# The first chunk of the projections taken in two halves of its tokens, with four weight blocks begun before the rounds

## The chip, the cores and the metric

The kernel runs on one core of a Trainium2 chip. The metric is the device time of one execution in microseconds (us), the median of several runs. Engines are named as the profile names them: PE multiplies matrices (PEld is its weight load), ACT applies functions and copies, DVE and POOL work element by element, SP only issues transfers. Each engine, and each queue of transfers, takes its instructions in the order in which they were written, and waits on semaphores for the others.

## The reference

One transformer block in float32, with S = 2048 tokens of D = 640, 32 heads of 20 and a gated layer of F = 1728:

```python
def _A_ref(x, wqkv, wo):
    qkv = (x @ wqkv).reshape(B, S, 3, H, Dh).transpose(2, 0, 3, 1, 4)
    q, k, v = qkv[0], qkv[1], qkv[2]
    p = softmax(einsum("bhqd,bhkd->bhqk", q, k) * Dh ** -0.5)
    return einsum("bhqk,bhkd->bhqd", p, v).transpose(0, 2, 1, 3).reshape(B, S, D) @ wo
def _B_ref(x, w_gate, w_up, w_down):
    return (silu(x @ w_gate) * (x @ w_up)) @ w_down
h  = x + _A_ref(layernorm(x), wqkv, wo)
h2 = h + _B_ref(layernorm(h), w_gate, w_up, w_down)
```

The layer norm has no weights: `(x - mean) / sqrt(var + 1e-5)`.

## The kernel before, in words

**Stages.** The projections (q, k, v) take the first 320 us, attention follows until about 1430 us, and the gated layer fills the rest. All engines' instructions are laid down in program order (`manual_schedule`); nothing is reordered later.

**Precision.** A float32 operand is held as two fast-format parts, `hi` (a copy by ACT) and `lo` (the difference, by DVE or POOL); `split` makes them. A product is the sum of three: `z_hi·w_hi`, `z_lo·w_hi`, `z_hi·w_lo`, so a weight block of 128 columns needs 15 steps (three parts by `ND` = 5 slices of D).

**Projections.** Tokens go in four chunks of 512 (`CH`), each of four tiles of 128 (`TPC`). A chunk has 18 work items: ten blocks `("block", m)` of 128 columns (even m are keys, odd m queries) and eight value parts. `slot` counts work items, 18 per chunk, 72 in all. In `rounds`, a block's matmuls are cut into a half over rows 0 to 63 and a half over rows 64 to 127; the second halves follow 20 steps behind (`LAG`), so that in the steady state two halves run side by side. `keep` takes a finished block out of PSUM: ACT copies, DVE or POOL takes the difference, the result `e` is stored to DRAM (`q_d`, `k_d`) through POOL's queue (`store`); for the last block of the last chunk through SP's queue.

**Row maxima in between.** Softmax needs each row's maximum. Part of them is computed during the projections (`early`, from `items` that are loaded back from DRAM with `load_items`, by SP's queue): `max_four` multiplies, ACT takes a relu, PE adds, DVE reduces. `visit`, called after each step of `rounds`, decides from modelled engine clocks (`clock`, `takes`, `held`, `given`) whether one of these goes in. `stored_at` says from which slot on a group's keys and queries count as stored.

**The hand-over to attention.** Unit 0 is the first of 32 (head group, query chunk) units. When the last of its maxima is reduced, `max_all(0)` puts `neg` in place. Two work items later, or behind the last one when the items run out, `max_finish(0)` transposes `neg` on PE, splits it (ACT, then DVE: tile `m`) and lets SP write it into rows of `q_stk` by four transfers (L352). The first score of attention (L1297) reads those rows.

**The first chunk.** `load_x(0)` loads the four token tiles, then `load_w` the weights, 256 columns (two blocks) each, into a ring of four `raw` tiles. `norm(0)` computes mean and variance of all four tiles (DVE, L137, L138), the reciprocal root by a bit trick and three Newton steps (`rstd_steps`, L111), and normalises each tile (L574). Meanwhile PE multiplies a tile by the identity three times (`warm`, L820). `flip_tokens` transposes a tile on PE (L628) and splits it into `z_hi`, `z_lo`. `first_blocks` then computes blocks 0 and 1 with full-height matmuls over 256 tokens (L720), and `rounds` begins with block 2 (L667).

## Time and profile before

| | |
|---|---|
| median of 3 runs | 2004.37 us (2004.31 to 2004.98) |
| the profiled execution: its time | 2004.65 us |
| its span, first to last instruction | 2002.9 us, so 1.75 us lie around it |
| PE busy | 1981.1 us, 99% |
| DVE, ACT, POOL busy | 1604.4, 1430.4, 786.2 us |
| granted clock of TensorE | 0.999 |

A line of a timeline reads: start in us from the span's start, duration in us, engine, source line, operation, output<-inputs, shape, number of merged instructions; in brackets the idle time of the engine just before and what ended it. A line without brackets followed its predecessor at once. Lines of SPq are the issues of transfers by SP's queue. For merged rows the duration runs from the start of the first to the end of the last. Line numbers are those of the kernel before; in the changed kernel the same line stands a few to some sixty lines further on.

### The profile page before, as it was taken

The page shows a single profiled execution, that of the slowest core. Times are in us where ns is not written, and L with a number is a line of the kernel's source. Part 1 is how long each engine was busy: PE and PEld are TensorE (multiplying, and loading weights), DVE is VectorE, ACT ScalarE, POOL GpSimd, SP SyncE. Part 2 cuts the span into 40 slices and gives each one's busy share as a digit, 9 for nine tenths or more (in the row PEclk, how much of TensorE's full clock was granted, in tenths as well). Part 3 has the DMA queues.
Part 4 walks back from the last instruction along what each step waited for, and adds up shares of the span by engine and source line. Part 5 has one row for each costly group of instructions (what it writes and reads, how often), then busy time and mean ns, then how long its engine had stood idle before and what let it go on. Part 6 is the DMA issues. An engine that isn't in the chain of part 4 may idle for free.

```text
span 2002.9 us, 41974 instructions
## 1 busy us (share of the span) xinstructions
PE 1981.1 (99%) x14792; PEld 1260.4 (63%) x14792; DVE 1604.4 (80%) x2873; ACT 1430.4 (71%) x2828; POOL 786.2 (39%) x1152
## 2 busy tenths in 40 slices
PE   8999999999999999999999999999999999999998
PEld 6999996444444444444444444455688888888887
DVE  5687778999999999999999999975478666677667
ACT  4677778999999999999999999977633221212221
POOL 6564423243252343334342111011255544844465
PEclk9999999999999999999999999999999999999999
DMA  7787563442533544435345222221268645974542
GB/s 239 258 258 258 176 208 90 129 121 97 161 104 114 150 135 130 130 111 157 120 134 161 79 73 60 77 67 59 65 207 291 235 159 180 358 243 166 199 147 93
DMA packets 197066, 310.50 MB, mean 155 GB/s; under 512 B 51368, under 2 KB 85480, under 8 KB 195832
## 3 DMA queue, kind: packets, MB, share of 16 engines
q1 hardware_dynamic: 190264, 284.21, 43.9%
q0 software_dynamic: 6496, 23.60, 3.9%
q8 instruction: 118, 1.93, 0.4%
q14 instruction: 92, 0.75, 0.1%
q10 hardware_dynamic: 96, 0.00, 0.0%
HBM read 208.11 MB, written 99.19 MB: 153 GB/s over the span
## 4 chain that ended last, share of the span: by engine, by line
PE 90%; DVE 1%; POOL 1%; ACT 1%; DMA 1%; issue 0%; SPq 0%; DVEq 0%; POOLq 0%; ACTq 0%
PE acc L1307 25%; PE ps_a L1494 15%; PE ps_one L1297 12%; PE ps_max L289 9%; PE ps_b L1588 8%; PE ps_max L261 7%; PE ps_one L667 7%; PE ps_max L228 3%; PE ps_max L1028 2%; PE ps_b L1028 1%; DMA t_d<-kept 0%; POOL h L1626 0%; DVE tmp L1709 0%; PE ps_max L1063 0%; POOL yp L102 0%
## 5 line engine op out<-in xcount | busy, mean ns | idle before, releaser
L1303 ACT ACTIVATE probs<-ps_one 128x512 f32<-128x512 f32 x2048 | 1049.2, 615 | 43.0 <-PE ps_one L1297 33.9
L267 DVE TENSOR_REDUCE found<-ps_max 128x1 f32<-128x512 f32 x980 | 630.4, 685 | 81.1 <-PE ps_max L261 63.7
L1297 PE MATMUL ps_one<-q_stk,k_stk 62*128 62x512 f32 x2048 | 571.9, 427 | 0.2 <-ACT probs L1303 0.2
L1307 PE MATMUL acc<-probs,v_stk 128*32 128x512 f32 x4096 | 546.6, 605 | 0.0
L289 PEld LDWEIGHTS ps_max<-k_stk,q_stk 60*128 60x128 f32 x984 | 181.8, 185 | 407.1 <-DVE found L267 402.7
L261 PE MATMUL ps_max<-k_stk,q_stk 60*128 60x512 f32 x980 | 392.9, 422 | 0.0
L298 DVE TENSOR_REDUCE found<-ps_max 128x2 f32<-128x512 f32 x492 | 335.1, 681 | 0.0
L289 PE MATMUL ps_max<-k_stk,q_stk 60*128 60x256 f32 x984 | 324.1, 329 | 0.0
L1297 PEld LDWEIGHTS ps_one<-q_stk,k_stk 62*128 62x128 f32 x2048 | 301.7, 184 | 20.0 <-ACT probs L1303 16.2
L1709 DVE TENSOR_TENSOR tmp<-ps_a,tmp 128x512 f32<-128x512 f32 x208 | 141.1, 689 | 119.7 <-PE ps_a L1494 94.0
L250 DVE TENSOR_REDUCE mx<-ps_max 128x2 f32<-128x512 f32 x288 | 180.7, 685 | 69.1 <-PE ps_max L228 61.8
L261 PEld LDWEIGHTS ps_max<-k_stk,q_stk 60*128 60x128 f32 x980 | 181.0, 185 | 52.1 <-DVE found L298 21.6
L1588 PE MATMUL ps_b<-halves,yp 128*128 128x320 f32 x1032 | 179.3, 308 | 2.0 <-POOL yp L102 1.2
L240 ACT ACTIVATE ps_max<-ps_max 128x512 f32<-128x512 f32 x288 | 151.4, 584 | 40.9 <-PE ps_max L228 38.9
L1588 PEld LDWEIGHTS ps_b<-halves,yp 128*128 128x128 f32 x1032 | 165.1, 188 | 18.7 <-POOL yp L102 1.5
L1494 PE MATMUL ps_a<-t,units 128*128 128x512 f32 x624 | 162.6, 396 | 0.0
L1307 PEld LDWEIGHTS acc<-probs,v_stk 128*32 128x32 f32 x4096 | 81.0, 108 | 128.5 <-issue 118.3
L102 POOL TENSOR_TENSOR yp<-y,yp 128x256 fp32r<-128x256 f32 x96 | 60.2, 627 | 188.2 <-ACT yp L101 188.2
L1494 PE MATMUL ps_a<-z,units 128*128 128x512 f32 x516 | 133.9, 394 | 0.0
L1494 PEld LDWEIGHTS ps_a<-t,units 128*128 128x128 f32 x624 | 112.5, 188 | 18.6
L1342 POOL TENSOR_TENSOR o<-o,rb 128x512 f32<-128x512 f32 x31 | 39.8, 1285 | 212.1 <-DMA q_stk<-q_d 80.0
L319 POOL CAST both<-neg 128x16 fp32r<-128x16 f32 x22 | 4.3, 197 | 299.0 <-DVE neg L309 243.5
(220 smaller groups left out, 3077.3 us busy)
## 6 DMA issues: line engine op xcount, KB each, us to landing
units<-w_d SPq DMA_DIRECT2D x186, 256.0 KB
w_d<-stage SPq DMA_DIRECT2D x106, 256.0 KB
halves<-j_d SPq DMA_DIRECT2D x70, 320.0 KB
j_d<-stage SPq DMA_DIRECT2D x42, 320.0 KB
k_stk<-k_d SPq DMA_DIRECT2D x64, 160.0 KB
q_stk<-q_d SPq DMA_DIRECT2D x64, 160.0 KB
raw<-k_d SPq DMA_DIRECT2D x62, 160.0 KB
raw<-q_d SPq DMA_DIRECT2D x54, 160.0 KB
```

The lines of the kernel that those rows point to most:

```text
L240: nc.scalar.activation(ps, ps, AF.Relu)
L250: nc.vector.tensor_reduce(mx[:, b, :, t, kc], ps.rearrange("p (j n) -> p j n", j=2), axis=AX.X, op=ALU.max,)
L261: nc.tensor.matmul(ps, queries[u][rows, pair, t * P : (t + 1) * P], keys[u // NC][rows, pair, kc * CH : (kc + 1) * CH], start=True, stop=True,
L267: nc.vector.tensor_reduce(found_of(u)[:, b, pair, t, kc : kc + 1], ps, axis=AX.X, op=ALU.max)
L289: nc.tensor.matmul(ps[:, b * CH // 2 : (b + 1) * CH // 2], queries[u][rows, pair, t * P : (t + 1) * P], keys[u // NC][rows, pair, first : ...
L298: nc.vector.tensor_reduce(found_of(u)[:, :, pair, t, column], ps.rearrange("p (b n) -> p b n", b=2), axis=AX.X, op=ALU.max,)
L1297: nc.tensor.matmul(ps, keys[u // NC][rows, p, kt * P : (kt + 1) * P], queries[u][rows, p, :], start=True, stop=True,)
L1303: nc.scalar.activation(probs[p][:, b, :], ps, AF.Exp, scale=scale)
L1307: nc.tensor.matmul(acc[32 * j : 32 * j + 32, :], values[u // NC][:, kt, j * VW : j * VW + 32], probs[j // 2][:, j % 2, :], start=(kt == 0) ...
L1494: nc.tensor.matmul(ps.rearrange("p (t n) -> p t n", t=TPC), w[k][:, i], z[k][:, :, j], start=(first and m == 0), stop=(last and m == len(n ...
L1588: nc.tensor.matmul(ps, a, b, start=(n == 0), stop=(n == len(pairs) - 1))
L1709: add = lambda out, ps, x: nc.vector.tensor_tensor(out=out, in0=ps, in1=x, op=ALU.add)
```

## The change: what it does

It rewrites the first chunk's beginning and what depends on it:

- SP loads token tiles 0 and 1, then the first weights, then tiles 2 and 3, then the other weights. The matmuls by the identity are two instead of three and read tile 1.
- Statistics, reciprocal root and normalisation go by pairs of tiles (`first_tokens`), with `scalar_tensor_tensor` on two tensors (a constant tile `magic`, `r` broadcast along the row) where `norm` has `tensor_scalar`. For the other chunks `norm` stays as it is.
- Blocks 0 to 3 (not 0 and 1) are computed by `first_blocks`, with 256 tokens per matmul: for tokens 0 to 255 as soon as tiles 0 and 1 are flipped, for tokens 256 to 511 in work item 0. Blocks 2 and 3 have two PSUM banks of their own, a pool on the other side (`psum_pair`); `psum_wide` shrinks from three buffers to two. `rounds` begins with block 4.
- The `lo` parts of weight blocks 0 to 3 are made by POOL (before: DVE), and POOL's fill of `k_stk` with ones (L153) comes behind them, no longer first.
- The planner: `stored_at` is `2 * block + 5` for chunk 0, `given` starts with one entry, work items 2 and 3 of chunk 0 are empty, and each pair of first blocks advances PE's modelled clock by 3510 ns.

```diff
-        for c, name, n in ((ps_ctx, "psum_o", 2), (flip_ctx, "psum_w", 3))
+            (ps_ctx, "psum_o", 2, "left"), (flip_ctx, "psum_w", 2, "left"),
+            (pair_ctx, "psum_p", 1, "right"),
...
-                return 2 * block + 4 + (block > 0)
+                return 2 * block + 5
...
-        given = [0, 0, 0]
+        given = [0]
...
+        def first_tokens(ts, mv):
+            n = len(ts)
+            v, r, t = (pa.tile([P, n], F32, name=f"{x}_first", bufs=2) for x in "vrt")
+            var = mv[:, ts[0] : ts[-1] + 1, 1]
+            stt = nc.vector.scalar_tensor_tensor
+            stt(v, var, EPS, var, op0=ALU.add, op1=ALU.max)
+            stt(r.bitcast(I32), v.bitcast(I32), -0.5, magic[:, :n], op0=ALU.mult, op1=ALU.add)
+            for _ in range(3):
+                nc.vector.tensor_tensor(out=t, in0=r, in1=r, op=ALU.mult)
+                stt(t, t, -0.5, v, op0=ALU.mult, op1=ALU.mult)
+                stt(r, t, 1.5, r, op0=ALU.add, op1=ALU.mult)
+            for i, k in enumerate(ts):
+                stt(
+                    xs[k], xs[k], mv[:, k, 0:1], r[:, i : i + 1].to_broadcast([P, D]),
+                    op0=ALU.subtract, op1=ALU.mult,
+                )
...
-        load_x(0)
-        fill_ones(k_stk[0])
-        for i in range(4):
+        load_x(0, 0, 2)
+        load_w(0)
+        load_x(0, 2, TPC)
+        for i in range(1, 4):
             load_w(i)
         warm = ps_one()
-        for _ in range(3):
-            nc.tensor.matmul(warm, ident, xs[TPC - 1][:, :CH], start=True, stop=True)
-        for _, _, f in norm(0):
-            f()
+        for _ in range(2):
+            nc.tensor.matmul(warm, ident, xs[1][:, :CH], start=True, stop=True)
...
+        def first_low(*ms):
+            for m in ms:
+                cs = slice(m * P, (m + 1) * P)
+                nc.gpsimd.tensor_tensor(
+                    out=w_lo[:, :, cs], in0=first_raw[m], in1=w_hi[:, :, cs].bitcast(F32),
+                    op=ALU.subtract,
+                )
...
+        first_high(0, 1)
+        first_low(0, 1)
+        first_stats(0)
+        first_stats(1)
+        first_tokens((0, 1), moments)
+        first_stats(2)
+        flip_tokens(0)
+        flip_tokens(1)
...
+        first_high(2, 3)
+        first_low(2, 3)
+        fill_ones(k_stk[0])
+        first_blocks((0, 1), (0, 0), (0, 1), (0, 2))
+        first_stats(3)
+        first_tokens((2, 3), moments)
+        first_blocks((2, 3), (0, 0))
+        flip_tokens(2)
+        first_blocks((2,), (0, 1))
+        flip_tokens(3)
+        first_blocks((3,), (0, 1))
+        first_blocks((2, 3), (0, 2))
...
-        first = [("block", 0), ("none",)] + [("block", m) for m in range(2, 2 * ND)]
+        first = [("block", 0), ("none",), (), ()] + [("block", m) for m in range(4, 2 * ND)]
...
-                        first_blocks((0, 1), (1, 0), (1, 1), (0, 2), (1, 2))
-                        for m, ps in enumerate(firsts):
-                            keep(0, m, ps)
+                        for ms in ((0, 1), (2, 3)):
+                            first_blocks(ms, (1, 0), (1, 1), (1, 2))
+                            takes("PE", 3510)
+                            for m in ms:
+                                keep(0, m, firsts[m])
```

**Where instructions move: PE, start of the program.** `L628` and `L631` are the transposes of token tiles, `L720` and `L721` are `first_blocks`, `L667` and `L670` are `rounds`. Before:

```order
L820 MATMUL ps_two<-xt,ident 128x512 x3
L628 MATMUL ps_wide<-ident,xt 128x128 x15
L720 MATMUL ps_two<-z_hi,w_hi 128x256 x10
L628 MATMUL ps_wide<-ident,xt 128x128 x5
L720 MATMUL ps_two<-z_lo,w_hi 128x256 x10
L720 MATMUL ps_two<-z_hi,w_hi 128x256 x10
L720 MATMUL ps_two<-z_lo,w_hi 128x256 x10
L720 MATMUL ps_two<-z_hi,w_lo 128x256 x20
```

Now, to the end of the first half of blocks 2 and 3:

```order
L840 MATMUL ps_two<-xt,ident 128x512 x2
L631 MATMUL ps_wide<-ident,xt 128x128 x10
L721 MATMUL ps_two<-z_hi,w_hi 128x256 x10
L721 MATMUL ps_two<-z_lo,w_hi 128x256 x10
L721 MATMUL ps_two<-z_hi,w_lo 128x256 x10
L721 MATMUL ps_pair<-z_hi,w_hi 128x256 x10
L631 MATMUL ps_wide<-ident,xt 128x128 x5
L721 MATMUL ps_pair<-z_lo,w_hi 128x256 x5
L631 MATMUL ps_wide<-ident,xt 128x128 x5
L721 MATMUL ps_pair<-z_lo,w_hi 128x256 x5
L721 MATMUL ps_pair<-z_hi,w_lo 128x256 x10
```

Forty matmuls now stand between the transposes of tiles 0 and 1 and those of tile 2; sixty more, over the second half of the tokens, follow these rows.

**PE, the hand-over to attention.** `ps_max<-raw` are the maxima computed from loaded items, `ps_max<-ident,neg` is the transpose in `max_finish(0)`, and `ps_one<-q_stk` is the first score, which before is the row behind the last one shown. Before:

```order
L345 MATMUL ps_max<-ident,neg 16x128
L667 MATMUL ps_one<-z_hi,w_lo 128x512 x5
L667 MATMUL ps_one<-z_hi,w_hi 128x512
L228 MATMUL ps_max<-raw 128x256 x4
L667 MATMUL ps_one<-z_hi,w_hi 128x512
L228 MATMUL ps_max<-raw 128x256 x4
L667 MATMUL ps_one<-z_hi,w_hi 128x512 x3
L667 MATMUL ps_one<-z_lo,w_hi 128x512 x3
L228 MATMUL ps_max<-raw 128x256 x4
L667 MATMUL ps_one<-z_lo,w_hi 128x512 x2
L667 MATMUL ps_one<-z_hi,w_lo 128x512 x5
L289 MATMUL ps_max<-k_stk_145,q_stk 128x256
```

Now:

```order
L670 MATMUL ps_one<-z_lo,w_hi 128x512
L670 MATMUL ps_one<-z_hi,w_lo 128x512 x5
L231 MATMUL ps_max<-raw 128x256 x4
L348 MATMUL ps_max<-ident,neg 16x128
L292 MATMUL ps_max<-k_stk_148,q_stk 128x256
L1362 MATMUL ps_one<-q_stk,k_stk_148 128x512
```

The transpose of `neg` stood twenty steps of `rounds` and three groups of maxima ahead of the first score; now one short matmul stands between the two, behind the last step of the projections.

**SP's queue at the same place.** `q_d<-e` stores the last block of queries, `q_stk<-m` are the four transfers of `max_finish(0)`, `m` being the split transpose. Before:

```order
L181 DMA v_stk_146<-v_d 128x16x96
L352 DMA q_stk<-m_5529 1x8x128 x4
L639 DMA q_d_62<-e_170 48x2x512
L639 DMA q_d_62<-e_170 80x2x512
L164 DMA q_stk<-q_d_62 40x1024
```

Now:

```order
L184 DMA v_stk_149<-v_d 128x16x96
L642 DMA q_d_62<-e_173 48x2x512
L642 DMA q_d_62<-e_173 80x2x512
L355 DMA q_stk<-m_5596 1x8x128 x4
L167 DMA q_stk<-q_d_62 40x1024
```

The two stores of the last block have moved ahead of the four transfers that the first score reads.

More of the change, by code (lines that the diff above doesn't have):

```diff
@@ L708, in finish_splits, with first_blocks @@
                 splits.pop(0)[1]()
-        def first_blocks(*hns):
-            if not firsts:
-                firsts.extend(ps_one() for _ in range(2))
+        def first_blocks(ms, *hns):
             z_hi, z_lo = zs[0]
@@ L823, in tile_block @@
         zs[0] = z_tiles(0)
[L824 to L835 removed]
+        first_raw = {}
@@ L901, in ps_max @@
                         three[0] += 1
-                        return psum.tile([P, CH], F32, name="ps_max", tag=f"ps_max{three[0] % 3}")
+                        return max_bank(three[0])
                 if c == 0 and j == 6:
@@ L956, in ps_max @@
         place[0] += 1
-        return psum.tile([P, CH], F32, name="ps_max", tag=f"ps_max{place[0] % 3}")
+        return max_bank(place[0])
     pp = att_ctx.enter_context(tc.tile_pool(name="pp", bufs=6, side="right"))
```

62 lines of the change are left out of this document (37 added, 25 removed).

## The prediction

> **What bounds the kernel now.** I read the page's busy times and its chain first, then the timeline of the first 50 us on every engine, then the place where the projections hand over to attention, with SP's waits.
>
> ```profile
> span 2002.9 us, 41974 instructions
> PE 1981.1 (99%) x14792; PEld 1260.4 (63%) x14792; DVE 1604.4 (80%) x2873; ACT 1430.4 (71%) x2828; POOL 786.2 (39%) x1152
> PE 90%; DVE 1%; POOL 1%; ACT 1%; DMA 1%; issue 0%; SPq 0%; DVEq 0%; POOLq 0%; ACTq 0%
> PE ps_two L820 <- DMA xt<-in_A_x: 7.5, 1, 7.5
> PE ps_b L1588 <- POOL yp L102: 1.2, 1, 1.2
> ```
>
> The last two rows are PE's longest waits: 7.5 us at the start, and nothing over 1.2 later. PE bounds the whole program, and the change leaves its matmuls nearly as they are. So the time moves by two things only: when PE's useful work begins, and new stretches in which PE waits. The profiled execution took 2004.65 us (span 2002.9 and 1.75 around it), 0.28 above the median 2004.37; the sum is made against 2004.65. I treat 0.2%, 4 us, as the least difference that can be told from no change.
>
> ```profile
> 3.61 0.89 DVE L137 BATCH_NORM_STATS2 st<-xt 128x6 f32<-128x320 f32 x2 [2.73 <-DMA xt<-in_A_x]
> 5.52 0.21 DVE L138 BATCH_NORM_AGGREGATE mv<-st 128x2 f32<-128x12 f32 x1
> 7.49 5.46 PE L820 MATMUL ps_two<-xt,ident 128*128 128x512 f32 x6 [7.49 <-DMA xt<-in_A_x]
> 8.54 0.17 DVE L111 TENSOR_SCALAR v_a<-mv 128x4 f32<-128x4 f32 x1
> 9.25 1.36 ACT L826 ACTIVATE w_hi<-raw 128x640 fp32r<-128x640 f32 x2 [7.22 <-DMA raw<-in_A_wqkv]
> 11.34 2.26 DVE L574 TENSOR_SCALAR xt<-xt,mv,r_a 128x640 f32<-128x640 f32 x4
> 12.74 1.94 PE L628 MATMUL ps_wide<-ident,xt 128*128 128x128 f32 x15
> 13.62 1.90 ACT L101 ACTIVATE z_hi<-ps_wide 128x640 fp32r<-128x640 f32 x3 [3.01 <-PE ps_wide L628]
> 14.98 1.44 PE L720 MATMUL ps_two<-z_hi,w_hi 128*128 128x256 f32 x10 [0.30 <-ACT z_hi L101]
> 17.99 1.34 PE L720 MATMUL ps_two<-z_hi,w_hi 128*128 128x256 f32 x10
> 19.16 1.34 PE L720 MATMUL ps_two<-z_lo,w_hi 128*128 128x256 f32 x10
> 19.95 3.02 DVE L102 TENSOR_TENSOR w_lo<-raw,w_hi 128x640 fp32r<-128x640 f32 x4
> 22.79 1.43 PE L667 MATMUL ps_one<-z_hi,w_hi 64*128 64x512 f32 x5
> 27.95 9.19 POOL L102 TENSOR_TENSOR w_lo<-raw,w_hi 128x640 fp32r<-128x640 f32 x6
> ```
>
> Useful work on PE begins at 12.74, behind 5.2 us of multiplying by the identity, and from 14.98 it runs on without a bracket. Ten matmuls over 256 tokens take 1.17 us (17.99 to 19.16), 0.117 each.
>
> **Part 1, the front: −1.0 us.** As a common mark I take the point where blocks 0 to 3 are done. Before, rounds begin at 22.79 with two of these left; two blocks are 2 × 30 × 0.117 = 7.0, so the mark is 29.8. Now: statistics of tiles 0 and 1 end as before, at 5.73. Eleven small operations follow, at the step of before, (11.34 − 8.54)/14 = 0.20: to 7.9. Operations on two tensors of 640 columns take 3.02/4 = 0.76 (normalising cost 2.26/4 = 0.57): tiles 0 and 1 stand at 8.7 and 9.5. Five transposes (0.65) and a copy (0.7) later, at 11.0, PE starts on forty matmuls, 4.7 us, to 15.7. DVE meanwhile: z_lo of tile 1 to 11.8, statistics of tile 3 to 12.9, eleven small ones to 15.1, tile 2 to 15.9, tile 3 to 16.6. PE is back at 16.0, needs 1.3 for transposes, 2.3 for twenty matmuls and 7.0 for sixty, and reaches the mark at 26.7: a gain of 3.1 if nothing collides.
>
> Two things collide. POOL now makes four `lo` parts in this stretch, 9.19/6 = 1.53 each; the first can begin when ACT has its `hi` part, near 8.1 (two tiles of 328 KB fewer are loaded ahead of the first weights; at the 355 GB/s below that is 1.9 us less than 9.25, and 0.7 for ACT), just when DVE normalises tiles 0 and 1. Elsewhere the trace shows what happens then:
>
> ```profile
> 1495.07 0.69 DVE L1713 TENSOR_TENSOR tmp<-tmp 128x512 f32<-128x512 f32 x1
> 1517.11 1.82 DVE L1713 TENSOR_TENSOR tmp<-tmp 128x512 f32<-128x512 f32 x1
> 1517.10 1.29 POOL L102 TENSOR_TENSOR kept<-zz,kept 128x512 fp32r<-128x512 f32 x1 [1.23 <-ACT kept L101]
> ```
>
> The same DVE operation takes 0.69 alone and 1.82 when POOL began 0.01 earlier: it sat out POOL's 1.29. I count one such wait before tile 1 (1.5) and up to two in the chain for tiles 2 and 3 (2.1): mark at 30.3, 0.5 late. [...] The other thing is PE's speed.
>
> ```profile
> 325.85 1.07 PE L1307 MATMUL acc<-probs,v_stk 128*32 128x512 f32 x8
> 7.50:12.70 5.20, 5.20 (x6) 1.00 1.10 355
> ```
>
> The six records by the identity start 0.86 apart (5.46 over six, less the tail of the last); in attention eight records of the same length and type, four column groups side by side and two in a row each, take 1.07. So the early records run at about half speed, and they did so for 5.2 us, though the second row (a stretch: PE busy, granted clock, DMA share, GB/s) gives a granted clock of 1.00. Now there are four such records (3.4 us), then gaps: the forty matmuls may run at up to twice 0.117, 4.7 more, though 2 or so of that lies beside DVE's chain. Between 26.7 and 31 I take 28.8: −1.0.
>
> **Part 2, blocks 4 on: +0.5 us.** POOL carried seven operations less ahead of the weights; now it fills `k_stk` and makes four `lo` parts first. That still ends by about 23, hidden. But stores of block 2 and 3 now come ahead of the `lo` parts of block 6 on, and SP's raw tiles become free only behind these.
>
> ```profile
> 39.78 1.65 POOL L639 DMA_DIRECT2D q_d<-e  x3
> 31.49 1.97 SPq L414 DMA_DIRECT2D xt<-in_A_x  x4
> 34.11 1.86 SPq L164 DMA_DIRECT2D raw<-k_d  x4
> 51.34 2.15 SPq L164 DMA_DIRECT2D raw<-q_d  x4
> 47.91 0.40 PE L228 MATMUL ps_max<-raw 60*128 60x256 f32 x4
> ```
>
> From the mark on: keep of block 2 and its stores to +5.0, those of block 3 (1.65) to +6.7, block 6's `lo` at +8.2; PE asks for it at +9.4 (twenty unpaired half steps of 0.234, then 20 pairs). The loads for the first maxima go out from +12.9 (before +4.3) and land near +19.8; PE asks at +19.9 (before 47.91, +18.1). The second group's queries go out at +25.4 to 27.2 (before 51.34, +21.5), landing near +29, and PE asks between +27.2 and +29.5. So from 0 to 2.0; I take 0.5, since the first three just fit. SP's loads of the next tokens slip too, from 31.5 to about +10 past the mark, with DVE's statistics due at +9: a DVE wait of 2 to 3 us behind which one block's evacuation stands, covered by three banks of 3.5 us each; uncovered it would cost these 2 to 3.
>
> **Part 3, the hand-over: +7.1 us.**
>
> ```profile
> 317.08 0.25 ACT L101 ACTIVATE m<-ps_max 16x128 fp32r<-16x128 f32 x1
> 317.36 3.20 SPq L352 DMA_DIRECT2D q_stk<-m  x4
> 320.63 1.33 PE L667 MATMUL ps_one<-z_hi,w_lo 64*128 64x512 f32 x5
> 321.92 0.50 PE L1297 MATMUL ps_one<-q_stk,k_stk 62*128 62x512 f32 x1
> 322.04 0.60 ACT L752 ACTIVATE e<-ps_one 128x512 f32<-128x512 f32 x1 [2.10 <-POOL e L102]
> 322.67 0.63 ACT L101 ACTIVATE e<-e 128x512 fp32r<-128x512 f32 x1
> 323.39 1.27 POOL L102 TENSOR_TENSOR e<-e 128x512 fp32r<-128x512 f32 x1
> 324.69 0.80 SPq L639 DMA_DIRECT2D q_d<-e  x2
> SPq L639 <- POOL e L102: 4.0, 1, 4.0
> 350.45 2.75 SPq L352 DMA_DIRECT2D q_stk<-m  x4
> SPq L1336 <- DMA r_d<-r: 2.7, 2, 1.4
> ```
>
> Before, the four transfers of row maxima leave at 317.36, under PE's last matmuls, and the first score follows the last of these at 321.92 with no wait. The two stores behind them wait 4.0 us for POOL, and that costs nothing, as nobody stands behind them. In the changed queue the stores come first, so the four transfers, and with them the first score, stand behind POOL. From PE's last step, E = 321.96 on this clock: ACT's two copies to E + 1.34, POOL to E + 2.7, two stores to E + 3.5, four transfers of 2.75 to 3.20 to E + 6.3 to 6.7, and landing at most 1.36 (320.56 to 321.92), like the 1.4 of the wait for r_d: first score at E + 7.6 to 8.1. PE has only the last group of maxima and the transpose for it, some 0.5 us that were moved here; 0.2 comes back at the first exponentials, which ACT no longer delays. That gives 6.9 to 7.4; with a landing of 1.0 the lower end is 6.5. Taken: 7.1. Nothing later can return it, as PE waits for nothing in attention.
>
> **Part 4, speed behind the wait: +2.6 us.** At the start 7.5 us without work were followed by 5.2 us at half speed. Seven idle us here are nearest to that: 5.2/2 = 2.6; the least is 0, if only the start is slow. [...]
>
> Sum: 2004.65 − 1.0 + 0.5 + 7.1 + 2.6 = 2013.85, forecast 2013.8.
>
> **The rivals.** (a) The slow speed belongs to the start alone: no part 4, 2011.2. For it: the granted clock reads 1.00 throughout. Against: the one long idle time that the trace has was followed by half speed. (b) The front collides fully: mark at 31 and 2 us in part 2: 2004.65 + 1.2 + 2.0 + 7.1 + 2.6 = 2017.5. (c) Not slower: the hand-over is off PE's path. That is so if PE's tail is itself held until the four transfers land, by DVE's last reductions, or if the first score has other work ahead of it; it decides once 7 us of work or of older waiting stand between E and the score. Then parts 3 and 4 vanish: 2004.2, and with the whole gain of the front 2001.1. For it: the stores' wait of 4.0 harmed nobody. Against: a single short matmul stands there now, and PE was not held before.
>
> **How the numbers follow.** Forecast 0.50; (a) 0.22; (b) 0.14; (c) 0.14, of which 0.04 with the front's full gain. The forecast's own range is 2011 to 2016.5, from the ends of parts 1 to 4. The range for 8 in 10 takes in (a) with a gain of 3.1 at the front and a wait of 6.5 (2008.5 with part 2 at 0.5, 2008.0 at nothing) and (b): 2007.5 to 2018; (c) is left out. Slower by over 0.2% 0.82 (a little of (a) falls inside), within 0.2% 0.12, faster 0.06.
>
> **What the next profile would show.** Part 1: first useful matmul near 11 to 13 and blocks 0 to 3 done near 28.8; DVE operations of over 1.5 us there mean the collision. Part 2: PE waits of under 2 us on loaded tiles between 40 and 70. Part 3: one PE wait of about 7 us for the transfers of row maxima at 320 to 330, the longest after the start, and SP waiting for POOL at the stores. Part 4: matmuls at double spacing for some us behind it. A score that starts without that wait makes the prediction wrong.

## The result, and the profile after

The changed kernel takes 2029.53 us (median of four runs, 2027.93 to 2033.15) against 2004.67 of the kernel before in the same series: ratio 1.0123 (95% interval 1.0106 to 1.0141). It is slower by 25 us, where 9 were forecast. The profiled execution took 2030.12. The page's first rows:

```profile
span 2028.3 us, 41990 instructions
PE 1992.2 (98%) x14790; PEld 1270.4 (63%) x14790; DVE 1608.5 (79%) x2878; ACT 1432.4 (71%) x2828; POOL 794.5 (39%) x1156
```

The span grew by 25.4 us. PE is busy for 11.1 us more (1992.2 − 1981.1) with two matmul records fewer, so its matmuls ran slower; the other 14.3 are PE waiting. Three marks of the program, read in each kernel's timeline, put the loss in its place: the point where blocks 0 to 3 are done (in the kernel before the 29.8 that the prediction works out, as blocks 2 and 3 run inside `rounds` there), the end of the projections' last step, and the first score of attention.

| profiled execution | mark | mark to last step | last step to first score | first score to end |
|---|---|---|---|---|
| before | 29.8 | 292.2 | 0.0 | 1681.0 |
| after | 30.57 | 305.3 | 7.75 | 1684.7 |
| difference | +0.8 | +13.1 | +7.8 | +3.7 |
| predicted | −1.0 | +0.5 | +7.1 | +2.6 |

PE's longest waits up to the first score (engine, tile and line that waited, what released it: us in total, times, longest):

```profile
PE ps_one L1362 <- DMA q_stk<-m: 5.5, 1, 5.5
PE ps_two L840 <- DMA xt<-in_A_x: 4.7, 1, 4.7
PE ps_max L606 <- DVE xt L577: 3.9, 4, 2.1
PE ps_max L231 <- DMA raw<-q_d: 3.0, 2, 2.3
PE ps_max L231 <- ACT ps_max L243: 2.9, 5, 1.5
```

The wait at the start fell from 7.5 to 4.7, as the first matmuls now wait for the second token tile instead of the fourth. In its place stand the wait of 5.5 for the four transfers of row maxima at the hand-over, and about 10 us in the middle, of which the prediction had allowed at most 2, for loaded tiles: for normalised tiles of the second chunk (L606 is their transpose), for queries loaded back, and for ACT.

**The front** (start, duration, operation; DVE, POOL and PE):

```profile
8.12 2.97 DVE L739 SCALAR_TENSOR_TENSOR xt<-xt,mv,r_first 128x640 f32<-128x640 f32 x2
8.79 3.69 POOL L852 TENSOR_TENSOR w_lo<-raw,w_hi 128x640 fp32r<-128x640 f32 x2 [7.47 <-ACT w_hi L847]
13.91 3.08 POOL L852 TENSOR_TENSOR w_lo<-raw,w_hi 128x640 fp32r<-128x640 f32 x2 [1.43 <-ACT w_hi L847]
15.52 1.48 DVE L733 SCALAR_TENSOR_TENSOR r_first<-v_first,magic 128x2 int32<-128x2 int32 x1
18.80 1.68 DVE L739 SCALAR_TENSOR_TENSOR xt<-xt,mv,r_first 128x640 f32<-128x640 f32 x2
13.26 2.50 PE L721 MATMUL ps_two<-z_hi,w_hi 128*128 128x256 f32 x10 [0.79 <-ACT z_hi L104]
17.65 1.34 PE L721 MATMUL ps_two<-z_hi,w_lo 128*128 128x256 f32 x10
```

The normalising pair takes 1.68 where POOL makes no `lo` part but fills `k_stk` (the second pair, at 18.80) and 2.97 where POOL's first `lo` part begins inside it; one operation on two columns takes 1.48 beside POOL's later ones, where most take 0.16. The first twenty matmuls take 4.39 (13.26 to 17.65), half the pace of the ten behind them.

**The middle**, first SP's wait and the timeline of what hangs on it:

```profile
SPq L550 <- POOL w_lo L105: 14.8, 1, 14.8
```

```profile
37.10 9.19 POOL L105 TENSOR_TENSOR w_lo<-raw,w_hi 128x640 fp32r<-128x640 f32 x6
40.64 2.80 SPq L417 DMA_DIRECT2D xt<-in_A_x  x4
43.55 2.02 SPq L167 DMA_DIRECT2D raw<-k_d  x4
69.82 0.20 POOL L114 TENSOR_TENSOR r_a<-r_a,t_a 128x4 f32<-128x4 f32 x1
71.17 3.86 DVE L577 TENSOR_SCALAR xt<-xt,mv,r_a 128x640 f32<-128x640 f32 x4
72.16 0.37 PE L606 MATMUL ps_max<-ident,xt 64*128 64x64 f32 x2 [2.06 <-DVE xt L577]
```

All `lo` parts of the later weights (POOL, six at 37.10) begin 9.15 later than before (27.95), since the stores of four blocks stand ahead of them in POOL's queue. SP waits 14.8 for the first two of them, and behind that wait stand the loads of the next tokens (40.64, before 31.49) and the first loads back (43.55, before 34.11). POOL's last step of the reciprocal root for the second chunk falls at 69.82, and PE waits for the tile normalised behind it. In the kernel before the same three steps lie 13.32, 13.30 and 8.41 earlier:

```profile
56.50 0.20 POOL L111 TENSOR_TENSOR r_a<-r_a,t_a 128x4 f32<-128x4 f32 x1
57.87 3.86 DVE L574 TENSOR_SCALAR xt<-xt,mv,r_a 128x640 f32<-128x640 f32 x4
63.75 0.65 PE L603 MATMUL ps_max<-ident,xt 64*128 64x64 f32 x14
```

What PE did there, in stretches (length, then busy us and count of PE, PEld, DVE, ACT, POOL, granted clock, DMA share, GB/s; the first row is the kernel before, the others the changed one):

```profile
60.00:80.00 20.00, 19.04 (x284) 18.54 (x284) 13.03 (x21) 14.91 (x31) 12.00 (x15) 1.00 0.79 288
60.00:80.00 20.00, 13.60 (x128) 12.32 (x127) 8.28 (x12) 7.31 (x14) 11.80 (x23) 0.74 0.76 251
62.90:65.20 2.30, 0.03 (x2) 0.06 (x2) 0.00 (x0) 0.02 (x1) 2.15 (x3) 1.00 0.67 204
65.40:68.60 3.20, 3.20 (x29) 3.20 (x29) 0.00 (x0) 2.16 (x5) 2.82 (x4) 0.50 0.88 229
70.10:72.20 2.10, 0.04 (x2) 0.04 (x2) 2.06 (x4) 0.00 (x0) 0.00 (x0) 1.00 0.95 340
72.20:78.90 6.70, 4.88 (x42) 4.32 (x44) 2.76 (x3) 1.83 (x4) 2.24 (x3) 0.50 0.63 230
```

Two waits of 2.3 and 2.1 are each followed by a stretch at a granted clock of 0.50. In it one pair of half-height matmuls over 320 columns follows the last after 0.27 us (L670 at 76.06, 76.33, 76.59); at 1.00 it is 0.15 (68.87, 69.02, 69.17). Of PE's 13.60 us of work in these 20 us, 3.20 + 4.88 were done at 0.50. Counted by the clock they are worth 4.04, by the pace of the pairs 4.45; both are estimates. By the first that is 9.56 us of work at full clock, where the kernel before fits 19.04 and e7 below 19.29, and these 20 us alone hold 9.5 of the 13.1 lost in the middle (9.1 by the second).

**The hand-over**:

```profile
336.05 0.28 PE L348 MATMUL ps_max<-ident,neg 128*16 128x128 f32 x1
338.60 0.78 SPq L642 DMA_DIRECT2D q_d<-e  x2
339.43 2.94 SPq L355 DMA_DIRECT2D q_stk<-m  x4
343.63 0.76 PE L1362 MATMUL ps_one<-q_stk,k_stk 62*128 62x512 f32 x1 [5.50 <-DMA q_stk<-m]
```

```profile
343.60:352.00 8.40, 8.34 (x35) 4.25 (x39) 5.35 (x9) 5.72 (x12) 2.10 (x1) 0.50 0.16 57
352.00:354.00 2.00, 2.00 (x20) 0.92 (x16) 1.16 (x3) 1.19 (x3) 0.00 (x0) 0.98 0.00 0
```

The last step ends at 335.88, the two stores leave behind POOL at 338.60, the four transfers at 339.43, and the first score starts at 343.63. Then PE works for 8.4 us at half clock.

### The profile page after: what moved, and what is told of

Same layout as the page of the kernel before. It is cut to its first block, busy times and chain, and to the rows that moved or that the text cites. A ratio compares the mean times of both kernels' runs of the same rounds, so it can differ in the third digit from the quotient of the medians.

```text
span 2028.3 us, 41990 instructions
## 1 busy us (share of the span) xinstructions
PE 1992.2 (98%) x14790; PEld 1270.4 (63%) x14790; DVE 1608.5 (79%) x2878; ACT 1432.4 (71%) x2828; POOL 794.5 (39%) x1156
## 4 chain that ended last, share of the span: by engine, by line
PE 85%; DMA 1%; DVE 1%; POOL 1%; ACT 1%; issue 0%; SPq 0%; DVEq 0%; POOLq 0%; ACTq 0%
PE acc L1372 25%; PE ps_a L1559 15%; PE ps_one L1362 12%; PE ps_max L292 9%; PE ps_b L1653 8%; PE ps_max L264 7%; PE ps_one L670 4%; PE ps_max L1093 2%; PE ps_max L231 1%; PE ps_b L1093 1%; DMA halves<-j_d 0%; DMA units<-w_d 0%; SPq L1318 0%; PE ps_max L1128 0%; DVE tmp L1774 0%
```

## The experiments

The kernel changed is the one after, unless a line says otherwise; ratios are to the kernel before. All marks of the table above, for the runs that are compared:

| | median us | ratio (95%) | mark | mark to last step | to first score | to the end |
|---|---|---|---|---|---|---|
| e1 | 2025.05 | 1.0100 (1.0085 to 1.0115) | 29.9 | 305.7 | 1.7 | 1685.5 |
| e2 | 2029.25 | 1.0123 (1.0107 to 1.0139) | 31.1 | 302.2 | 7.7 | 1684.6 |
| e3 | 2036.63 | 1.0153 (1.0136 to 1.0170) | 34.6 | 309.8 | 7.7 | 1685.0 |
| e4 | 2013.78 | 1.0042 (1.0027 to 1.0057) | – | – | 7.7 | 1683.4 |
| e5 | 2025.21 | 1.0095 (1.0079 to 1.0111) | 30.9 | 301.8 | 7.7 | 1682.5 |
| e6 | 2016.90 | 1.0059 (1.0044 to 1.0074) | 29.2 | 303.1 | 1.7 | 1683.1 |
| e7 | 2008.66 | 1.0017 (1.0007 to 1.0026) | 30.9 | 291.7 | 1.7 | 1683.6 |
| e8 | 2011.19 | 1.0028 (1.0017 to 1.0039) | 29.9 | 291.1 | 1.7 | 1682.5 |
| e9 | 2014.98 | 1.0046 (1.0031 to 1.0062) | 30.7 | 298.1 | 0.1 | 1683.6 |
| e10 | 2011.49 | 1.0034 (1.0022 to 1.0045) | 30.0 | 296.5 | −0.2 | 1683.6 |
| e11 | 2008.61 | 1.0020 (1.0011 to 1.0028) | 28.3 | 296.1 | −0.2 | 1684.5 |
| e12 | 2006.52 | 1.0008 (0.9999 to 1.0017) | 27.9 | 291.2 | 1.7 | 1683.6 |
| e13 | 2004.38 | 0.9999 (0.9990 to 1.0008) | 28.3 | 291.0 | 2.1 | 1681.3 |
| e14 | 2013.02 | 1.0039 (1.0024 to 1.0054) | – | – | 7.8 | 1682.5 |

The stages are those of one profiled execution each, which for e8 lies 4 us under its median (2006.96), for e3 2.4 above and elsewhere within 2. e4 and e14 are the kernel before with an edit and have no such mark.

### e1_finish_early: the transpose of `neg` one work item earlier

```diff
-                    finish_at = min(finish_at, slot[0] + 2)
+                    finish_at = min(finish_at, slot[0] + 1)
```

> The changed kernel, in which the transpose of the maxima and its four transfers go one work item earlier, so that they stand about 20 steps of the last block ahead of the first score again and ahead of the last block's two stores on SP. Theory (the hand-over costs what its wait and the half speed behind it take): the 5.5 us and 1.4 us waits go, and so does the granted clock of 0.50 from 338 to 352 us; 7.1 for the wait and (352.0 - 343.6)/2 = 4.2 for the speed: 2029.5 - 11.3 = 2018.2 (2016.5 to 2020). Rival 1 (the slow speed does not hang on this wait): only 7.1 comes back, 2022.4, and 340 to 360 still shows a clock near 0.7. Rival 2 (something else is late there, such as the last maxima or the loads behind the four transfers): 2027 to 2030, with another wait of 5 us or more in the same place.

The wait for the transfers is gone: the first score starts 1.7 us after the last step instead of 7.75. But the time fell by 4.5 only, to between the two rivals. The last group of row maxima is still reduced behind the last step, and PE waits for it:

```profile
337.24 0.38 PE L292 MATMUL ps_max<-k_stk,q_stk 60*128 60x256 f32 x1 [1.34 <-DVE found L280]
```

Behind these 1.34 us the clock reads 0.50 from 338 to 344.7. So the hand-over's wait was the transfers, as predicted, and a slow stretch does not need a wait of that length.

### e2_split_early: weights of blocks 6 and 7 split ahead of the stores

```diff
-        split_at = (0, 4, 6, 7, 8, 9, 10, 11, 12, 13)
+        split_at = (0, 6, 6, 7, 8, 9, 10, 11, 12, 13)
```

> The changed kernel, in which weight blocks 6 and 7 are split (ACT and POOL) ahead of the keeping of blocks 0 to 3, no longer behind it; nothing else moves. Theory (POOL's stores of four blocks held the raw tile that SP's last weight load waited for, 14.8 us, and all later loads slid behind it): the load goes out near 27.5 instead of 40.2, the next tokens near 28 to 31 instead of 40.6, transfers no longer stand still at 22 to 26 us, PE's waits of 2.3 (loaded queries) and 3.9 (normalised tiles) at 62 to 75 go, and with them the granted clock of 0.50 there (3.3 and 3.9 us of work at half speed, 3.6): 2029.5 - 6 - 3.6 = 2020 (2018 to 2022.5). Rival 1 (the next chunk's normalisation was late by its own order on POOL and DVE, behind stores and reductions): the 3.9 and half of the slow speed stay, 2024 to 2026. Rival 2 (PE's waits at 62 to 75 come from the planner's item order): no change, 2028 to 2030.

The time did not change (2029.25). The next tokens' load went out at 28.32 instead of 40.64, and the wait for loaded queries fell from 3.0 to 0.3. The wait for normalised tiles grew:

```profile
PE ps_max L606 <- DVE xt L577: 5.5, 4, 3.5
```

Its last step of the reciprocal root still ran on POOL at 67.90 (before 56.50). An earlier landing did not help, so I took the lateness to have a second source, in the order itself: `takes("PE", 3510)` advances the planner's clock twice ahead of the second chunk's load, where before only block 2, about 3.5 us, had passed by then. The normalisation, due a fixed time after its load on that clock, is laid 3.5 us later among the steps, while its transposes keep their work item.

### e3_scalar_norm: first normalisation by `tensor_scalar`, as before

```diff
-                stt(
-                    xs[k], xs[k], mv[:, k, 0:1], r[:, i : i + 1].to_broadcast([P, D]),
+                nc.vector.tensor_scalar(
+                    xs[k], xs[k], mv[:, k, 0:1], r[:, i : i + 1],
```

> The changed kernel with the four normalisations of whole tiles by tensor_scalar again (the eleven small operations stay on two tensors). Theory (POOL's two lo parts shut the two-tensor operation out): the first pair takes 2 x 0.57 = 1.15 instead of 2.97, the second 1.15 instead of 1.68; blocks 0 to 3 are done near 28.5 instead of 30.6, and the time is 2029.5 - 1.8 = 2027.7 (2026.5 to 2028.8). Rival (a tensor_scalar is slowed as much beside POOL, and what counts is only that both run together): 2029 to 2030, the first pair still near 3 us.

2036.63 us, ratio 1.0153 (1.0136 to 1.0170); the mark moved from 30.57 to 34.61, and the middle took 4.5 more. My theory, that the operation on two tensors was the poorer choice, is wrong. The first pair gained 0.6 (2.37 instead of 2.97), but the second lost 4.2, as it now sits beside POOL's fill of `k_stk`:

```profile
17.68 5.90 DVE L739 TENSOR_SCALAR xt<-xt,mv,r_first 128x640 f32<-128x640 f32 x2
15.93 7.30 POOL L156 MEMSET k_stk<- 32x4096 f32 x2
```

5.90 us for what takes 1.68 by two-tensor operations in the same place. The pair ends at 23.58, 0.35 behind the end of the fill (23.23). The traces show both operations beside both kinds of POOL's work: on two tensors 1.68 for two beside a fill and 2.97 beside a `lo` part, as `tensor_scalar` 5.90 and 2.37. With POOL idle four `tensor_scalar` take 2.26 (the kernel before, at 11.34). Why the `tensor_scalar` is held by a fill and the operation on two tensors is not, no run shows.

### e4_before_late_finish: the kernel before, with its hand-over made late

```diff
-                    finish_at = min(finish_at, slot[0] + 2)
+                    finish_at = min(finish_at, slot[0] + 20)
```

> The kernel before, in which only the transpose of the maxima and its four transfers go behind the last work item, as in the changed kernel. Theory: PE waits about 7 us there and works about 8 us at half speed behind it: 2004.7 + 7.1 + 4.2 = 2016.0 (2014 to 2017.5). Rival 1 (half speed belongs to something else in the changed kernel): 2011.8. Rival 2 (the queue has time enough here, as the last maxima were reduced earlier): 2004.5 to 2006.

This is parts 3 and 4 of the prediction by themselves, in the kernel before: +8.4 us (2013.78 against 2005.41 in its series), a little under the range that the theory gave.

```profile
328.30 0.76 PE L1297 MATMUL ps_one<-q_stk,k_stk 62*128 62x512 f32 x1 [5.48 <-DMA q_stk<-m]
```

The first score comes 7.73 after the last step, which itself comes 1.4 earlier than before (320.56 against 321.96). So of the span's 8.8 the start of attention holds 6.4 and the half-clock stretch behind it (328.3 to 336.6) 2.4; that stretch had been put at 4.2.

### e5_split_and_norm_early and e6_three_moves: the causes of the middle together, then with e1

```diff
-        split_at = (0, 4, 6, 7, 8, 9, 10, 11, 12, 13)
+        split_at = (0, 6, 6, 7, 8, 9, 10, 11, 12, 13)
...
-                    x_there[0] = clock["PE"] + X_LANDING
+                    x_there[0] = clock["PE"] + X_LANDING - (0 if c else 3510)
```

> The kernel of e2 (blocks 6 and 7 split ahead of the keeping), in which the planner also takes the next tokens as landed 3.51 us earlier, by as much as the new line for PE's modelled clock put them later; the steps of the next chunk's normalisation then stand in DVE's and POOL's queues about where they stood in the kernel before. Theory (the middle loss is the planner's: normalisation steps were set 3.5 us later while the flips that need them kept their place, and each step lost another place behind reductions that wait for loaded maxima): the wait of 5.5 us for the normalised tiles that e2 still had goes, and the slow clock of 60 to 80 us (0.83, some 3.4 us): 2029.3 - 8 = 2021 (2019 to 2024). Rival (PE then waits as long for the loaded queries and keys, which come 7 us later after the mark than before): 2026 to 2029, with waits on DMA of 3 us or more at 50 to 65.

> e5 and e1 together: blocks 6 and 7 split ahead, normalisation steps earlier, the transpose of the maxima one work item earlier. If the gains add: 2021 - 4.5 = 2016.5 (2014 to 2019), with the 1.3 us wait for the row maxima of DVE and the slow clock behind it still there at the hand-over. If earlier maxima in the middle also bring the last maxima forward, that wait goes too and with it the slow speed behind: 2011 to 2013.

e5's last step of the root moved to 62.16 (after 69.82) and was still late: DVE waits 1.6 for it with two tiles to normalise, PE 2.4 behind that for a bank of maxima, and the other two tiles (70.05) stand in DVE's queue behind reductions that wait for PE, which costs PE another 2.4. POOL still carried `lo` parts and stores of all blocks between its Newton steps. e5's middle is only 0.4 shorter than e2's (301.8 and 302.2). e6 gets from e1's edit at the hand-over what e1 got, 6.0. The medians of e5 and e6 differ by 8.3, the two profiled executions by 5.8 (2024.71 and 2018.90); the front is 1.7 shorter in e6 and the middle 1.4 longer, though that edit touches neither, so differences of this size lie within the spread of runs.

### e9_dve_splits_alone and e7_dve_splits: POOL's load taken away

e9 makes the `lo` parts of blocks 4 to 9 on DVE, in work item 0, ahead of all stores; e7 does that on top of e6.

```diff
-        LATE, CHAIN = 6, 3000
+        LATE, CHAIN = 10, 3000
...
-        split_at = (0, 4, 6, 7, 8, 9, 10, 11, 12, 13)
+        split_at = (0, 8, 8, 8, 8, 9, 10, 11, 12, 13)
```

> e6, in which blocks 6 to 9 are split ahead of the keeping and their lo parts are made by DVE, which stood idle for 16 of the 20 us from 20 to 40. Theory (POOL's lo parts of 8 and 9, behind its stores, hold the raw tiles that the loads for the first maxima wait for, 12.3 us in e2): the first loads go out near 35 instead of 41.4, and 1 to 3 us of waits at 50 to 65 and at 120 to 140 go: e6 less 2. Rival (the first maxima are placed by the planner's times and find their loads late or early all the same): equal to e6 within 1 us, or up to 1 us slower by DVE's delay of the first evacuation.

> The changed kernel with one edit alone: blocks 6 to 9 are split ahead of the keeping of blocks 0 to 3, their lo parts by DVE (as in e7); normalisation steps and the transpose of the maxima stand as in the changed kernel. Theory (the whole middle loss is POOL's backlog: four blocks' stores ahead of lo parts, which hold SP's loads and POOL's own normalisation steps): the waits and the slow clock of 60 to 80 go as in e7, about 9.5 there and 1.6 at 120 to 140, and the hand-over stays: 2029.5 - 11 = 2018.5 (2016 to 2020.5). Rival (the planner's later steps of normalisation are needed as well, and e7's gain came from both): 2021 to 2025, with a wait of 2 us or more for normalised tiles left.

e7 gained 8.2 on e6 where 2 were expected. Stretch of e7, then of e9, and what e9 still waited for:

```profile
60.00:80.00 20.00, 19.29 (x285) 18.72 (x282) 14.56 (x23) 15.49 (x32) 13.06 (x14) 1.00 0.81 284
```

```profile
60.00:80.00 20.00, 18.18 (x239) 17.54 (x238) 13.05 (x20) 13.07 (x26) 11.45 (x13) 0.91 0.76 250
```

```profile
PE ps_max L606 <- DVE xt L577: 1.7, 2, 1.0
```

In e7 the stretch is full, at clock 1.00, and mark to last step is 291.7 (before 292.2): the middle's loss is gone whole. e9 recovers 7.2 of 13.1; the corrected planner's clock, together with e1's edit, recovers the other 6.4. So POOL's queue was about half and the later edits the rest; which is larger, single profiles do not say (the runs of e9 go from 2010.09 to 2016.60), and no run has the planner's edit without e1's on top of e9. e9 came out under both of its ranges, because the hand-over's wait went with it. In e9 the hand-over needed no edit at all: with less lateness the last maxima fell one group earlier and the first score followed the last step at 0.1. Its clock still fell to 0.50, from 331.65 to 338.49, with no wait ahead of it, which I cannot explain.

### e8_front_dve: the `lo` parts of blocks 2 and 3 on DVE as well

```diff
-        first_low(2, 3)
...
         first_blocks((3,), (0, 1))
+        first_low(2, 3, engine=nc.vector)
         first_blocks((2, 3), (0, 2))
```

POOL makes those of blocks 0 and 1, as in the changed kernel. On top of e7:

> e7, in which the lo parts of blocks 2 and 3 are made by DVE behind the tokens' splits, no longer by POOL beside DVE's statistics. Theory (the two small operations on two tensors that took 1.07 and 1.49 us sat out POOL's lo parts): they take 0.2 each, tiles 2 and 3 are normalised near 16.9 instead of 19 to 20.5, PE has no gap there, and blocks 0 to 3 are done 1.5 to 2.5 us earlier, if PE is not slowed by gaps between 8 and 13: e7 less 2. Rival (the next lo part that PE needs is late instead): a wait of 1 to 2 us for w_lo at 20 to 23 and no gain.

The collision is gone (the small operations take 0.16, the second pair is normalised by 17.7) and a wait of PE for `w_lo` took its place, as the rival said:

```profile
19.50:21.30 1.80, 0.04 (x1) 0.00 (x0) 1.57 (x3) 1.80 (x4) 0.44 (x1) 1.00 0.00 0
```

The mark came 1.0 earlier than in e7; the median did not gain (2011.19 against 2008.66). This wait of 1.80 was not followed by a lower clock (rows in the last section).

### e10_maxima_before, e11_fill_first and e12_plan_and_front: the front cleared

All three move the ten matmuls of the first tokens that wait for `w_lo` of blocks 2 and 3 behind the twenty with `w_hi` of the second tokens. e10 and e11 also count keys and queries of blocks 2 and 3 as stored from slot 5 on (in the changed kernel from slot 7). e11 and e12 bring POOL's fills (`k_stk` and the value tiles) to the program's start.

```diff
-        first_blocks((2, 3), (0, 2))
...
-                            first_blocks(ms, (1, 0), (1, 1), (1, 2))
+                            first_blocks(ms, (1, 0), (1, 1), *([(0, 2)] if ms[0] else []), (1, 2))
```

> e8, in which the second half of blocks 2 and 3 begins without their lo parts (the twenty matmuls with w_lo go behind those with w_hi of the second tokens), and blocks 2 and 3 count as stored from slot 5 on, since they are kept in slot 0; the last group of maxima then stands ahead of the last steps of the projections, as in the kernel before. Theory: the 1.8 us wait for w_lo goes, and at the hand-over the 1.3 us wait for DVE's last row maxima with the slow clock behind it (324 to 330, 2.5 to 3): from e8's profiled 2007.0 to 2002 (2000.5 to 2005), against 2004.7 of the kernel before. Rival 1 (maxima taken one group earlier wait for their loads at 45 to 60): 2005 to 2008. Rival 2 (the front of the changed kernel is a lottery of transfers and clock, from 2006 to 2013 in e7 and e8): a median of 2005 to 2009 with runs spread over 5 us or more.

> e10, in which POOL fills k_stk and the two ev tiles with ones at the start of the program, ahead of the lo parts of blocks 0 and 1, so that these begin near 9.8 and no more beside DVE's normalisation of tiles 0 and 1 (8.2 to 9.9). Theory (the spread of runs comes from that collision, 1.3 us when the weights land before 8.9, and from the slow clock that the longer gap brings, 2 us): median 1 to 2 us below e10, and runs within 3 us of each other. Rival (the spread is the clock's own, from the gaps of PE between 8.5 and 13, which stay): the same median and spread as e10 within 1 us.

> e8 with the front of e11 (POOL fills k_stk and ev at the program's start; the twenty matmuls with w_lo of blocks 2 and 3 over the first tokens go behind those with w_hi over the second), and the planner's numbers as in e8, so that the wait of 1.7 us and the slow clock of e11 at 100 to 120 should not come. Theory (the changed front gains 1.6 us once POOL, DVE and the clock leave it alone, 28.3 against 29.8, and e8's middle loses nothing): e8's profiled 2007.0 less (29.9 - 28.3) = 2005.4; with the slow clock behind the hand-over (2.5) still in it: 2004 to 2007, runs within 4 us of each other. Rival (the gain of the front is given back in the middle, since the planner's steps count from PE's modelled clock and not from the mark): 2007 to 2010.

With the fills first the mark is 28.3 and 27.9: the front's gain, 1.5 to 1.9 us, exists once nothing collides. e10 came out above all its ranges (2011.49), e11 was 2.9 better than e10 with its runs within 3.7, e12 as its theory had it. The `stored_at` of e10 and e11 closed the hand-over (first score with the last step) and opened a wait of 1.7 at 100 to 120 for ACT, in e11 with a slow stretch behind it (109.76 to 113.18). And with no wait at the hand-over, the clock of both still fell at attention's start, as in e9. e11:

```profile
324.80:328.21 3.41, 3.12 (x13) 1.30 (x10) 3.01 (x7) 3.38 (x8) 3.31 (x4) 1.00 0.66 170
328.21:331.63 3.42, 3.35 (x16) 1.59 (x16) 1.31 (x3) 2.07 (x5) 3.37 (x2) 0.50 0.87 250
```

e12, without it, is the same as before within its interval. Its last step comes at 319.11, 2.85 earlier than before, and that is given back: the wait of 1.3 for the last maxima, and then

```profile
319.40:320.70 1.30, 0.01 (x1) 0.01 (x1) 1.30 (x4) 1.02 (x2) 1.04 (x3) 0.93 0.64 136
320.70:322.00 1.30, 1.30 (x7) 1.30 (x8) 1.30 (x2) 0.17 (x1) 1.24 (x2) 0.50 0.87 249
327.30:330.00 2.70, 2.70 (x23) 1.27 (x20) 2.29 (x4) 2.55 (x6) 1.63 (x1) 0.99 0.01 3
```

1.3 us without matmuls, a clock of 0.50 from 320.51 to 327.34, then full.

### e13_fill_hand_over: the same wait, filled with matmuls that nobody reads

```diff
+        filler = ps_one()
+        for _ in range(2):
+            nc.tensor.matmul(
+                filler, ident, w_hi[:, 0, :CH].bitcast(F32), start=True, stop=True
+            )
```

> e12 with two multiplications by the identity (about 1.7 us of PE, results unused) behind the projections' last step, where PE otherwise waits 1.3 us for DVE's last row maxima. Theory (an idle stretch, even one of 1.3 us, lets the clock fall): no granted clock of 0.50 at 322 to 332, e12 less 2.5 plus 0.4 for the longer stretch: e12 less 2. Rival (the clock falls because of what runs there, single halves of 64 rows and then attention's first steps, not because of idle time; e9 fell to 0.50 at 331.8 with no wait over 0.3 near): e12 plus 0.4, with the clock at 0.50 as before.

```profile
319.39 1.98 PE L1007 MATMUL ps_one<-w_hi,ident 128*128 128x512 f32 x4
```

(two records for each of the two matmuls)

```profile
319.40:321.30 1.90, 1.90 (x5) 0.67 (x4) 1.29 (x2) 1.14 (x2) 1.64 (x3) 1.00 0.70 168
321.30:324.00 2.70, 2.38 (x15) 1.51 (x14) 2.49 (x6) 1.74 (x4) 2.64 (x2) 1.00 0.70 165
```

The first score is 0.5 later than in e12, the clock stays at 1.00, and the rest of the program takes 2.3 less: −2.1 in the medians. All eleven runs of e13 are shorter than e12's median. So in this pair the slow stretch came of PE's idle time. That attention's beginning can bring one with hardly any idle time, e9, e10 and e11 show (in e11 PE is busy for 3.12 of the 3.41 us ahead of it).

### e14_late_finish_filled: e4 with its longer wait filled

```diff
+        for _ in range(8):
+            nc.tensor.matmul(
+                filler, ident, w_hi[:, 0, :CH].bitcast(F32), start=True, stop=True
+            )
```

> e4 (the kernel before with the transpose of the maxima behind the last work item) with eight multiplications by the identity (about 6.9 us of PE, results unused) in PE's wait for the four transfers. The first score still waits as long. Theory (part 4 of the prediction: idle time costs its own length and the half speed behind it, 8.3 us long and worth 2.4): no granted clock of 0.50 at 323 to 337, e4 less 2.4: 2011.4 (2010.5 to 2012.5). Rival (the slow speed at the start of attention does not come from the wait): 2013 to 2014.5, clock as in e4.

2013.02 us, ratio 1.0039 (1.0024 to 1.0054): the time is the rival's, the clock is the theory's up to 331.7. It holds through the filled wait and the first scores, and falls a little later, behind a new wait:

```profile
320.90:327.90 7.00, 7.00 (x18) 2.89 (x17) 0.28 (x1) 1.38 (x3) 2.55 (x4) 1.00 0.57 152
331.70:336.30 4.60, 4.60 (x28) 2.24 (x32) 2.33 (x4) 2.69 (x6) 3.40 (x1) 0.63 0.02 4
```

```profile
331.66 0.38 PE L289 MATMUL ps_max<-k_stk,q_stk 60*128 60x256 f32 x1 [1.93 <-DVE found L298]
```

That matmul over the last maxima stood behind the filler in PE's queue, so its reduction came late too. The price of the slow stretch was moved, and the run does not settle it at this place; e13 does at its own.

## Why the prediction was wrong in size and right in sign

**Part 1, the front: −1.0 predicted, +0.8 measured**, inside the 26.7 to 31 that were given for the mark. Against the 26.7 worked out for no collision it is 3.9 late. The forty matmuls begin at 13.26 instead of 11.0: one collision in the first pair (1.3, of 1.5 counted), and transposes at half pace (1.33 for five instead of 0.65). The first twenty matmuls then cost 2.05 more (4.39 instead of 2.34), and PE had no idle time left between 13.26 and the mark to take that up. The collisions counted ahead of tiles 2 and 3 were smaller (one of 1.3, on two columns), and PE did not wait for them. So the term that was mis-sized is PE's pace: it was allowed for, but 2 us of it were laid beside DVE's chain, where PE did not wait. That pace is not fixed by the change: in e2, whose front has the same instructions, the same twenty matmuls take 2.48 (11.43 to 13.91), and a stretch at half clock follows later (19.16 to 22.57), so that its mark is no earlier. Of the 26 operations on two tensors that normalise the two pairs of tiles, two were held for over a us: 1.3 in the first pair's 2.97, and the one that took 1.48 instead of 0.16. e12 shows the size of the undisturbed gain: 1.9, not 3.1.

**Part 2, blocks 4 on: +0.5 predicted (0 to 2.0), +13.1 measured. This step failed.** The lateness of the transfers' issue was foreseen nearly to the us: loads for the first maxima "from +12.9" past the mark, 12.98 measured (43.55 − 30.57); the next tokens "about +10", 10.07 measured (40.64). What was wrong is where it was taken to end. The prediction followed the next tokens to their statistics and to one covered wait of DVE, and stopped there. It did not follow POOL's three Newton steps for them, which stand behind the same backlog in POOL's queue, nor the planner's 3.5 us, to the transposes that PE meets in a fixed work item: 71.17 for the normalised tile instead of 57.87, where the kernel before had its transpose only at 63.75, so 5.9 us of slack, from start to start, against 13.3 of delay. And it priced a wait as its length, though part 4 had a slow stretch behind a wait in hand: the two waits of 2.3 and 2.1 brought slow matmuls with them that cost about 4 us, by the estimate above. e9 and e7 show this: without the backlog 7.2 come back, with all of it mended the whole 13.1; e2, and e5 on top of it, take away parts and recover 3.1 and 3.5.

**Part 3, the hand-over: +7.1 predicted, +7.8 measured.** The first score at "E + 7.6 to 8.1" came at E + 7.75, and e4 repeats it in the kernel before (7.73). The 0.5 and 0.2 taken off for work moved there do not show in this distance; in e4 the last step came 1.4 earlier. Rival (c) is out, since nothing older stood before the score.

**Part 4, half speed behind it: +2.6 predicted, +3.7 measured**, of which e4 isolates 2.4. Rival (a), that the start alone is slow, is out: the granted clock reads 0.50 in rows behind the wait. What was mis-sized is the length of the slow stretch: 5.2 us of the start were carried over, 8.4 us of work were measured. The length is not in proportion to that of the wait: the clock was low for 13.65 us at the transfers' wait (338.43 to 352.09, the first 5.2 without work), and for 6.83 behind only 1.3 us in e12.

Rival (b) had the front's collision but only 2.0 for part 2; it stays 12 us below the result. The 2001.1 that (c) gives with the whole gain of the front takes the 1.0 of part 1 off twice (2004.65 − 3.1 + 0.5 is 2002.05); neither the forecast nor the range uses it.

What stays open: why the clock fell at attention's start in e9, e10 and e11 with no wait ahead; and whether a version exists that keeps the front's 1.5 to 1.9 us. The best here, e13, is the same as before (0.9990 to 1.0008): its last step comes 2.7 earlier, but the last group of maxima is then reduced behind it instead of under it.

## What to carry to other kernels

When a step moves into a queue, follow every item behind it to the last engine that waits, small vector steps included, and set its delay against the slack it had: here the transfers were placed right and the tile behind them was not followed. Before a wait of one or two us of a busy PE is priced at its length, read the granted clock of the stretch behind it: here such waits cost two or three times their length where the clock fell (4.4 us of waits and about 4 lost to slow work at 60 to 80; 1.3 and 2.3 at e12's hand-over), while behind the 1.80 of e8 it read 1.00. A gain at the front reaches the end only if what is planned in fixed work items, such as the last reduction before a hand-over, moves with it.

## What the runs showed of the hardware

- The granted clock of these runs changed in steps of 3.41 us. In the changed kernel its stretches at 0.50 lie at 65.37 to 68.78, 72.20 to 79.02 and 338.43 to 352.09, so they last 3.41, 6.83 and 13.65 us, and their ends are 0, 1, 2, 4, 80 and 84 steps of 3.413 from the first. In e9 and e12 the one at attention's start lasts 6.83, in e11 3.41.
- Two waits of about the same length had different outcomes; that their place in the steps decides is not shown. In the changed kernel, where one of 2.3 lay within a step, PE worked 0.90 us of the step that ends at 65.37, and the next step ran at half clock. The wait of 1.80 in e8 lay across an end (placed by counting back from e8's slow stretch, 324.45 to 327.86), PE worked 2.29 and 2.74 us of the two steps, and no slow step followed:

```profile
61.96:65.37 3.41, 0.90 (x7) 0.59 (x7) 0.10 (x1) 0.93 (x2) 2.81 (x7) 1.00 0.76 239
65.37:68.78 3.41, 3.41 (x30) 3.41 (x30) 0.07 (x1) 2.34 (x5) 3.00 (x4) 0.50 0.90 234
17.25:20.67 3.42, 2.29 (x20) 2.08 (x18) 2.23 (x4) 2.39 (x4) 2.69 (x1) 1.00 0.00 0
20.67:24.08 3.41, 2.74 (x22) 2.66 (x23) 3.41 (x5) 2.79 (x5) 0.00 (x0) 1.00 0.22 35
```

- Ahead of the changed kernel's three falls and of e12's PE worked for part of the step only: 0.90, 1.36 and 1.69 of 3.41 us, and 2.24 in e12 (317.10 to 320.51). That sets no limit: a wait of 1.7 in e10, at 100 to 120, was not followed by a fall (1.00 from 100 to 140), and at attention's start the clock fell behind steps with 3.18 in e9 and 3.12 in e11.
- The record of the granted clock does not show every slow stretch at the program's start: the twenty matmuls at 13.26 take 4.39 instead of 2.34 while it reads 1.00 over them.
- Two `tensor_scalar` of 640 columns took 5.90 beside a POOL fill and ended 0.35 behind it (e3), where two operations on two tensors took 1.68 beside the same fill (changed kernel, 18.80), as with POOL idle (e11, 16.14).
